# A chain of FNet and GeGLU layers on one core: two entries of the scheduler's machine picture are set in the source

## Chip, cores, metric

The kernel runs on one core of a Trainium2 chip. The metric is the device time of one execution, in microseconds; lower is better. Every program here is run several times, and the median counts.

The core's engines are TensorE (PE: matmuls; PEld: its weight loads), VectorE (DVE), ScalarE (ACT), GpSimd (POOL) and SyncE (SP, which issues transfers). Each works through its own queue in order and waits on semaphores for the others. Matmul results land in PSUM, of which this kernel uses 8 banks of 128 x 512; everything else on the core lies in SBUF.

## What is computed

An activation x of 2048 x 512 goes through four layers: FNet mixing, GeGLU, FNet mixing, GeGLU. All is float32.

```python
def _A_ref(x, dft_seq_re, dft_seq_im, dft_hid_re, dft_hid_im):
    a = jnp.einsum("bsd,ed->bse", x, dft_hid_re)
    b = jnp.einsum("bsd,ed->bse", x, dft_hid_im)
    return jnp.einsum("ts,bse->bte", dft_seq_re, a) - jnp.einsum("ts,bse->bte", dft_seq_im, b)

def _B_ref(x, w_gate, w_up, w_down):
    return (_gelu(x @ w_gate) * (x @ w_up)) @ w_down

x = x + _A_ref(_layernorm(x, axis=-1), A_dft_seq_re, A_dft_seq_im, A_dft_hid_re, A_dft_hid_im)
x = x + _B_ref(_layernorm(x, axis=-1), B_w_gate, B_w_up, B_w_down)
x = x + _A_ref(_layernorm(x, axis=-1), A_dft_seq_re, A_dft_seq_im, A_dft_hid_re, A_dft_hid_im)
x = x + _B_ref(_layernorm(x, axis=-1), B_w_gate, B_w_up, B_w_down)
```

The sequence matrices are 2048 x 2048, the hidden ones 512 x 512, and the feed-forward width is 1792.

## The kernel before

**Matmuls.** A float32 product is made of three reduced-precision ones. `split` (L137 to L139) cuts an operand into a high part, a copy on ACT (L138), and a low part, a subtraction on DVE (L139); `mm3` (L171 to L174) then adds high x high, high x low and low x high into one PSUM bank. So each 128 x 512 operand costs one ACT and one DVE instruction before its matmuls can run, the second matmul of three (or the third) needs the low part, and the first only the high part.

**Seven products for eight.** The big products are done on 2 x 2 blocks with seven block products (named A11, A12, S1 to S4 and A22 on one side, B.. and T1 to T4 on the other). This adds sums and differences on DVE (`plus` L163, `minus` L160), which work on loaded tiles before they are split and on PSUM banks when they are emptied. A bank is emptied by DVE (L163, adding to a tile) or by ACT (`copied`, L167); until then no later product may start in it.

**Tiles and loads.** 94 slots of 128 x 512 in SBUF hold everything in flight, with two wide tiles (`wide`, `xwide`) that are lent out as slots. SP issues nearly all loads in the order of its queue: the streamed matrices (L270, `ws` the sequence matrices, `wh` the hidden ones, `wc`, `wd`, `wdn` down weights), gate and up weights (`wgu` L845 to L847, their split copies `wb` L891), rows of x (L200, L209) and turned blocks `t` (L610). POOL issues the stores (L216, L227, L254, L863). A load into a slot waits until the last reader of the slot is done.

**Row statistics.** From the second layer on a row's mean and variance come from ACT (`norm_terms`: L492 sums a row, L493 the mean, L494 the squares), POOL (L495, L496) and ACT again (L497, and L514, which applies them). They share ACT's queue with the splits and the bank evacuations.

**What sets the order.** The source says what is done and in which program order, and which tile uses which slot. In what order each engine gets its instructions is decided by the tile framework's scheduler, which is called with `schedule_with_timeline_sim=True`: it plays the program through on a picture of the machine (a table of durations, the specification of the chip), and gives an engine that is free the first instruction in program order that is ready by that picture. The result is a fixed order for each queue, PE, ACT, DVE, POOL and SP alike. On the chip nothing of it is decided again: an instruction at the head of a queue that isn't ready holds up all behind it. Two entries of the picture matter here: `PE_FULL_CLOCK_PASS_GAP_NS`, the time between one pass over the array and the next beyond its columns, and `DGE_DMA_DELAY`, the time from the issue of a transfer to its start, with a value for each engine that issues.

Of the kernel before, what the change touches and what calls it, by code (L numbers as in the profile page):

```python
# [2 lines left out]

# [34 lines left out]
MADE = 5  # L38
LEAD = 3
NK = NS // 2  # L40


@with_exitstack
def fnet_geglu(ctx: ExitStack, tc: tile.TileContext, x_in, ws, wh, wgu, wdn, wdc, out):
# [153 lines left out]
    def x_load(layer, i, engine=nc.sync):  # L198
        t = sb.get()
        engine.dma_start(t, rows(layer, i))  # L200
        return t
# [116 lines left out]
    def make_a11(k):  # L318

        def run(v):  # L320
            held[k] = v
            return split_slot(v)
        return run
# [42 lines left out]
    def skewed(n):  # L366

        skew = SKEW[n - 2]
        return [(i, k - i * skew) for k in range(NK + (n - 1) * skew) for i in range(n) if 0 <= k - i * skew < NK]

# [14 lines left out]
    def bare(layer, b, what):  # L385

        return layer == 0 and b == 0 and what == "A11"
# [18 lines left out]
    def mix_items(layer):  # L406
        def raw(make, *tiles):
            items.append((F32, tiles, make, None))

        for b, what in plan(layer):  # L410
            tiles = [[ws[(b * 2 + m) * NS + k] for k in range(NS)] for m in range(2)]
            (a11, a12), (a21, a22) = ((r[:NK], r[NK:]) for r in tiles)
            hold = b >= FORE[layer]
            if what == "A11":
                for k in range(NK):
                    raw(as_is if bare(layer, b, what) else make_a11(k) if hold else plain, a11[k])
            elif what == "A12":
                for k in range(NK):
                    raw(plain, a12[k])
# [90 lines left out]
    def normed(layer, i, mixed=False):  # L510
        x = row_of(layer, i, mixed)
        z = sb.get()
        rstd, shift = known.pop((layer, i), None) or norm_terms(layer, i, x, z)
        nc.scalar.activation(z, x, AF.Identity, bias=shift, scale=rstd)  # L514
        sb.put(x)
        return z
# [11 lines left out]
    def first_rows(layer, k):  # L528
        for i in range(k if k == 0 else k + 2, min(k + 3, NK)):
            fresh[i] = x_load(layer, i)  # L530
        first_norm(layer, k)
        first_parts(k)

    def second_norm(layer, k):
        zb[k] = normed(layer, NK + k)

# [789 lines left out]
                geglu(w, layer)  # L1326


# [41 lines left out]
```

## Time and profile before

| | |
|---|---|
| runs shown | 1657.16, 1660.72, 1663.95 us (median 1660.72) |
| span of the profiled execution, first to last instruction | 1657.3 us |
| granted TensorE clock, mean | 0.994 |
| PE, PEld, DVE, ACT, POOL busy | 98%, 80%, 71%, 50%, 14% |
| matmuls of 128 x 512 in three parts | 2334 for each of the three lines of `mm3` |
| HBM read, written | 336.86 MB, 85.72 MB |

The profile is of one execution, and the time of that execution is its span and what lies around it, which the profile does not show; its span is as long as the shortest of the runs. Rows of the timeline give the start in microseconds, the duration, engine, line, operation, out<-in, and in brackets the idle time of the engine before it with what ended it. Names of tiles stand without their numbers: `p` is a PSUM bank, `s` a slot. "L163" is a line of the kernel, and often that of a helper, so many different sums share it. Records of matmuls overlap, so a matmul's duration in the profile is longer than the distance from its start to the next one's. A number in brackets behind a matmul is idle time only; time lost to a lower granted clock is read from tables of stretches.

### The profile page before, as it was taken

Reading aid. Unit: us, or ns where it says so; the run is one execution under the profiler, and the core shown is the slowest. Engines: PE = TensorE matmul, PEld = TensorE weight load, DVE = VectorE, ACT = ScalarE, POOL = GpSimd, SP = SyncE. Lnnn points to the kernel's source line nnn. Section 1 sums busy time; section 2 is a strip of 40 time slices with the busy share of each in tenths; the row PEclk is TensorE's granted clock in tenths of the full one; section 3 lists DMA queues with packets and bytes.
Section 4 is the critical chain, followed back from the end, with each engine's and each line's share of the span. In section 5 each row is a group of like instructions: output and inputs, shape, how many; then the busy total and the mean of one; then the engine's idle time right before and its main releaser. Section 6 shows DMA issues by size and latency. Waiting matters only on the chain.

```text
span 1657.3 us, 22815 instructions
## 1 busy us (share of the span) xinstructions
PE 1623.1 (98%) x7066; PEld 1329.5 (80%) x7066; DVE 1169.0 (71%) x2009; ACT 825.4 (50%) x1605; POOL 233.0 (14%) x421
## 2 busy tenths in 40 slices
PE   9999999989999999999999999999999999999998
PEld 6877888868788788888877888877778888788887
DVE  8998878769675674667877977787764556845573
ACT  7754454535675544555686433445345545523360
POOL 3111010202444113210030000101001000010002
PEclk9999999999999999999999999999999999999999
DMA  9768787789877799987867767777889775896455
GB/s 359 245 226 274 241 268 232 259 270 341 318 268 257 216 328 373 346 276 231 276 198 257 251 216 231 227 275 237 275 286 300 233 216 175 271 301 206 141 184 152
DMA packets 252106, 424.15 MB, mean 256 GB/s; under 512 B 28816, under 2 KB 91024, under 8 KB 250960
## 3 DMA queue, kind: packets, MB, share of 16 engines
q1 hardware_dynamic: 227232, 336.95, 63.9%
q0 software_dynamic: 24752, 85.74, 14.1%
q8 instruction: 56, 0.92, 0.2%
q14 instruction: 66, 0.54, 0.1%
HBM read 336.86 MB, written 85.72 MB: 255 GB/s over the span
## 4 chain that ended last, share of the span: by engine, by line
PE 76%; DMA 8%; DVE 7%; ACT 4%; issue 2%; SPq 1%; POOL 1%; DVEq 0%; ACTq 0%; POOLq 0%
PE p L172 25%; PE p L173 25%; PE p L174 25%; DVE s L139 3%; DMA s<-ws 3%; ACT s L138 2%; DVE s L160 2%; DMA s<-wgu 1%; DVE s L163 1%; DMA s<-x 1%; DMA s<-wdn 1%; DMA s<-t 1%; DMA t<-wide 0%; DMA begun<-wide 0%; ACT s L514 0%
## 5 line engine op out<-in xcount | busy, mean ns | idle before, releaser
L172 PE MATMUL p<-s,s 128*128 128x512 f32 x2334 | 891.6, 392 | 22.6 <-ACT s L138 8.4
L173 PE MATMUL p<-s,s 128*128 128x512 f32 x2334 | 911.3, 391 | 1.3 <-DVE s L139 1.3
L174 PE MATMUL p<-s,s 128*128 128x512 f32 x2334 | 901.0, 391 | 2.6 <-DVE s L139 2.5
L138 ACT ACTIVATE s<-s 128x512 fp32r<-128x512 f32 (+1 forms) x762 | 435.0, 606 | 452.6 <-DVE s L160 151.9
L139 DVE TENSOR_TENSOR s<-s,s 128x512 fp32r<-128x512 f32 (+1 forms) x762 | 483.2, 662 | 99.6 <-ACT s L138 77.7
L172 PEld LDWEIGHTS p<-s,s 128*128 128x128 f32 x2334 | 439.5, 188 | 122.6 <-ACT s L138 13.0
L174 PEld LDWEIGHTS p<-s,s 128*128 128x128 f32 x2334 | 440.2, 189 | 96.5 <-DVE s L139 3.8
L173 PEld LDWEIGHTS p<-s,s 128*128 128x128 f32 x2334 | 440.4, 189 | 94.5 <-DVE s L139 2.2
L163 DVE TENSOR_TENSOR s<-s,p 128x512 f32<-128x512 f32 x287 | 192.3, 682 | 169.9 <-PE p L174 74.1
L160 DVE TENSOR_TENSOR s<-s,s 128x512 f32<-128x512 f32 (+1 forms) x310 | 188.1, 620 | 47.3 <-DMA s<-ws 37.5
L167 ACT ACTIVATE s<-p 128x512 f32<-128x512 f32 x214 | 125.5, 592 | 113.5 <-PE p L174 105.9
L901 ACT ACTIVATE s<-s 128x512 f32<-128x512 f32 x103 | 64.6, 629 | 80.3 <-DVE s L163 79.4
L138 ACT ACTIVATE s<-xwide 128x512 fp32r<-128x512 f32 (+1 forms) x96 | 58.4, 615 | 46.9 <-DVE xwide L160 8.8
L163 DVE TENSOR_TENSOR s<-s,s 128x512 f32<-128x512 f32 (+1 forms) x70 | 43.0, 615 | 49.0 <-DMA s<-wgu 24.6
L495 POOL TENSOR_SCALAR rstd<-rstd 128x1 f32<-128x1 f32 x48 | 18.1, 378 | 406.7 <-ACT s L494 330.5
L139 DVE TENSOR_TENSOR s<-xwide,s 128x512 fp32r<-128x512 f32 (+1 forms) x96 | 64.5, 676 | 14.9 <-ACT s L138 12.7
L254 POOL DMA_DIRECT2D wb<-s x84 | 45.6, 545 | 56.4 <-ACT s L138 33.1
L915 DVE TENSOR_TENSOR s<-s,s 128x512 f32<-128x512 f32 x75 | 51.8, 690 | 1.9
L492 ACT ACTIVATE s<-s 128x512 f32<-128x512 f32 x39 | 24.4, 625 | 50.7 <-DMA s<-x 32.7
L514 ACT ACTIVATE s<-s,shift,rstd 128x512 f32<-128x512 f32 x55 | 43.9, 809 | 7.2 <-DVE shift L487 5.6
L216 POOL DMA_DIRECT2D x<-s x39 | 21.3, 546 | 171.8 <-DVE s L163 170.2
L596 DVE STREAM_TRANSPOSE wide<-s 128x512 f32<-128x512 f32 x30 | 21.1, 705 | 24.9 <-ACT s L514 19.3
(98 smaller groups left out, 530.7 us busy)
## 6 DMA issues: line engine op xcount, KB each, us to landing
s<-ws SPq DMA_DIRECT2D x379, 256.0 KB, 4.3
s<-wb SPq DMA_DIRECT2D x294, 256.0 KB, 4.8
s<-wc SPq DMA_DIRECT2D x119, 256.0 KB, 4.2
s<-wh SPq DMA_DIRECT2D x116, 256.0 KB, 4.3
wb<-s POOLq DMA_DIRECT2D x98, 256.0 KB, 4.5
s<-x SPq DMA_DIRECT2D x63, 256.0 KB, 5.0
xwide<-ws SPq DMA_DIRECT2D x58, 256.0 KB, 4.0
wc<-s POOLq DMA_DIRECT2D x49, 256.0 KB, 6.2
```

The source lines that it names most:

```text
L138: nc.scalar.activation(hi, src, AF.Copy)
L139: nc.vector.tensor_tensor(lo, src, f32(hi), op=ALU.subtract)
L160: nc.vector.tensor_tensor(out, a, b, op=ALU.subtract)
L163: nc.vector.tensor_tensor(out, a, b, op=ALU.add)
L167: nc.scalar.activation(v, src, AF.Copy)
L172: nc.tensor.matmul(ps, ah, bh, start=start, stop=False, skip_group_check=True)
L173: nc.tensor.matmul(ps, ah, bl, start=False, stop=False, skip_group_check=True)
L174: nc.tensor.matmul(ps, al, bh, start=False, stop=stop, skip_group_check=True)
L254: nc.gpsimd.dma_start(a, f32(t))
L514: nc.scalar.activation(z, x, AF.Identity, bias=shift, scale=rstd)
L901: nc.scalar.activation(t, g, AF.Gelu_apprx_tanh)
L915: nc.vector.tensor_tensor(t, t, v, op=ALU.mult)
```

## The change

While the scheduler orders the program, two entries of its picture are replaced, and put back afterwards: the gap between two passes of TensorE at full clock goes from 2.5 ns to 13.34 ns, and the delay of transfers issued by SP from 650 ns to 1900 ns (the other engines' stay as they are).

```diff
+PASS_GAP_NS = 13.34
+SP_DELAY_NS = 1900
...
+@contextmanager
+def machine_as_traced():
+
+    from concourse import hw_specs
+
+    spec = hw_specs.TRN2Spec
+    kept = {name: getattr(spec, name) for name in ("PE_FULL_CLOCK_PASS_GAP_NS", "DGE_DMA_DELAY")}
+    spec.PE_FULL_CLOCK_PASS_GAP_NS = PASS_GAP_NS
+    spec.DGE_DMA_DELAY = {**spec.DGE_DMA_DELAY, mybir.EngineType.SP: SP_DELAY_NS}
+    try:
+        yield
+    finally:
+        for name, value in kept.items():
+            setattr(spec, name, value)
...
-    with tile.TileContext(nc, schedule_with_timeline_sim=True) as tc:
+    with machine_as_traced(), tile.TileContext(nc, schedule_with_timeline_sim=True) as tc:
         fnet_geglu(tc, *ins, out)
```

The program has the same instructions on the same tiles and slots as before: 7,034 matmuls, 1,508 ACT, 2,009 DVE, 1,498 SP and 415 POOL instructions. Only their places in the queues differ. The lines of the kernel behind the two new constants are two further down than before, those from `kernel` on eighteen.

More of the change, by code (lines that the diff above doesn't have):

```diff
@@ L1 @@
 import math
-from contextlib import ExitStack
+from contextlib import ExitStack, contextmanager
 import concourse.bass as bass
```

## Prediction

> **What bounds the kernel now.** I read the page first: its span, the engines' busy shares, the chain that ended last, and the matmul groups.
>
> ```profile
> span 1657.3 us, 22815 instructions
> PE 1623.1 (98%) x7066; PEld 1329.5 (80%) x7066; DVE 1169.0 (71%) x2009; ACT 825.4 (50%) x1605; POOL 233.0 (14%) x421
> PE 76%; DMA 8%; DVE 7%; ACT 4%; issue 2%; SPq 1%; POOL 1%; DVEq 0%; ACTq 0%; POOLq 0%
> L172 PE MATMUL p<-s,s 128*128 128x512 f32 x2334 | 891.6, 392 | 22.6 <-ACT s L138 8.4
> L173 PE MATMUL p<-s,s 128*128 128x512 f32 x2334 | 911.3, 391 | 1.3 <-DVE s L139 1.3
> L174 PE MATMUL p<-s,s 128*128 128x512 f32 x2334 | 901.0, 391 | 2.6 <-DVE s L139 2.5
> ```
>
> TensorE is the bound. It makes 3 x 2,334 = 7,002 big matmuls and is idle for only 22.6 + 1.3 + 2.6 = 26.5 us in front of them. The mean of 391 ns is no pace, since records overlap; the pace is read from stretches. The next view is a table of stretches: its columns are PE, PEld, DVE, ACT and POOL busy with their instructions, then granted clock, DMA share and GB/s. The first row is undisturbed; the others begin where a stall had just ended.
>
> ```profile
> 200.00:250.00 50.00, 50.00 (x222) 41.41 (x221) 37.15 (x61) 24.66 (x55) 4.30 (x9) 1.00 0.80 270
> 349.00:353.00 4.00, 4.00 (x12) 3.14 (x11) 3.94 (x8) 1.71 (x4) 0.00 (x0) 0.57 0.56 163
> 372.80:376.20 3.40, 3.38 (x9) 2.64 (x10) 3.40 (x6) 1.42 (x3) 0.00 (x0) 0.55 1.00 329
> 430.20:434.60 4.40, 4.40 (x13) 3.46 (x14) 1.95 (x3) 1.26 (x3) 0.47 (x1) 0.61 0.68 238
> 542.30:547.20 4.90, 4.90 (x15) 3.86 (x16) 4.87 (x10) 3.34 (x7) 3.57 (x7) 0.65 1.00 270
> 870.90:878.00 7.10, 5.68 (x14) 4.16 (x15) 7.10 (x14) 7.10 (x15) 0.61 (x1) 0.54 0.48 153
> 1203.50:1207.00 3.50, 3.26 (x13) 2.39 (x14) 3.49 (x6) 0.63 (x1) 0.00 (x0) 1.00 0.88 309
> ```
>
> 50 us hold 222 matmuls, 225 ns each, so 7,002 of them need 1,577 us whatever their order. Behind five of the six long stalls the granted clock is 0.54 to 0.65 for some 4 us; one such drop costs (1 - 0.57) x 4.0 = 1.7 us. I use 1.7 us, and a chance of 5 in 6 that a stall of 1.9 us or more brings it. Five drops cost (1-0.57) x 4.0 + (1-0.55) x 3.4 + (1-0.61) x 4.4 + (1-0.65) x 4.9 + (1-0.54) x 7.1 = 10 us. A new order therefore has 26.5 + 10 = 36 us to win at most, 2.2% of the span, and no such limit on what it can lose.
>
> **The change part by part.** No instruction is added or removed. Comparing the two built programs instruction by instruction, 1,695 of 7,034 matmuls, 616 of 1,508 ACT, 910 of 2,009 DVE, 564 of 1,498 SP and 104 of 415 POOL instructions stand in another place of their engine's sequence, by 0.5 to 1.5 places in the mean. Queues run in order, so a moved instruction costs something only where its engine or its reader waits. I went through the stalls of TensorE one by one and took each engine's k-th place to be at the time of its k-th place before.
>
> Stalls that get shorter, in order of time:
>
> ```profile
> 95.28 0.50 PE L173 MATMUL p<-s,s 128*128 128x512 f32 x1 [1.03 <-DVE s L139]
> 483.54 0.73 PE L174 MATMUL p<-s,s 128*128 128x512 f32 x2 [0.99 <-DVE s L139]
> 542.25 0.50 PE L172 MATMUL p<-s,s 128*128 128x512 f32 x1 [2.66 <-DVE s L163]
> 870.88 0.75 PE L172 MATMUL p<-s,s 128*128 128x512 f32 x2 [3.46 <-ACT s L138]
> 873.05 1.22 PE L172 MATMUL p<-s,s 128*128 128x512 f32 x2 [1.42 <-ACT s L138]
> 1095.76 0.50 PE L172 MATMUL p<-s,s 128*128 128x512 f32 x1 [0.77 <-DVE s L163]
> 1415.22 0.50 PE L172 MATMUL p<-s,s 128*128 128x512 f32 x1 [0.56 <-ACT s L138]
> ```
>
> - 95.28: the low half waited for comes six places earlier on DVE, and the matmuls behind it go later: the whole 1.0 us.
> - 483.54: the two waiting matmuls move behind some fourteen that are ready: the whole 1.0 us.
> - 542.25: the evacuation waited for stands one place earlier, with one half-width subtraction less before it (two in 0.88 us, below): 0.4 us.
> - 870.88 and 873.05: the split waited for moves two places earlier on ACT, its low half one on DVE, and two matmuls of the second wait move back. Bounds 0 and 1.7 us (870.88 is 1.0 us earlier, and the next ready work 1.7); I take 0.7, because the second wait then begins sooner.
> - 1095.76: the evacuation (L163) moves one place forward, 0.6 us (five in 3.09 us at 1199.09, below).
> - 1415.22: two ready matmuls fill the gap: 0.5 us, and 0.3 us of a similar stall 6 us later.
>
> ```profile
> 540.72 0.88 DVE L160 TENSOR_TENSOR s<-s,s 128x256 f32<-128x256 f32 x2
> 541.52 0.68 DVE L163 TENSOR_TENSOR s<-s,p 128x512 f32<-128x512 f32 x1
> ```
>
> Together 1.0 + 1.0 + 0.4 + 0.7 + 0.6 + 0.5 + 0.3 = 4.5 us.
>
> Stalls that get longer. The first is at 137.40, where p waits for a PSUM bank that DVE empties with L163:
>
> ```profile
> 134.85 0.69 DVE L160 TENSOR_TENSOR s<-s,s 128x512 f32<-128x512 f32 x1 [1.00 <-DMA s<-ws]
> 136.66 0.68 DVE L163 TENSOR_TENSOR xwide<-s,p 128x512 f32<-128x512 f32 x1
> 137.40 0.50 PE L172 MATMUL p<-s,s 128*128 128x512 f32 x1 [1.31 <-DVE xwide L163]
> ```
>
> L163 moves three places back, behind three splits of other loads, at 0.60 us a place: 1.8 us. The bounds are 0.8 us (the 1.00 us that DVE idled at 134.85 is filled in the new order) and 1.8. I take 1.8, since two of those splits wait for loads of their own. The stall grows from 1.3 to 3.1 us, so a drop may follow: 5/6 x 1.7 = 1.4 us.
>
> The second is at 430.10. ACT empties two banks (L167) around a row statistic (L492) that waits for a load:
>
> ```profile
> 425.44 0.58 ACT L167 ACTIVATE s<-p 128x512 f32<-128x512 f32 x1
> 428.84 0.63 ACT L492 ACTIVATE s<-s 128x512 f32<-128x512 f32 x1 [2.19 <-DMA s<-x]
> 429.47 0.58 ACT L167 ACTIVATE s<-p 128x512 f32<-128x512 f32 x1
> 430.10 0.50 PE L172 MATMUL p<-s,s 128*128 128x512 f32 x1 [1.90 <-ACT s L167]
> ```
>
> In the new order the first L167 stands behind L492 as well, so it ends at 429.47 + 0.58 = 430.05, and the second goes behind the squares too. TensorE has six matmuls left from 424.6 on where it had thirteen: seven more are still to do at 430.1, 7 x 0.225 = 1.6 us. Late next are the six matmuls of that bank, which cover the second L167. The bounds are 0 (were the load early) and 2.6 (seven at the dropped clock, 3.40 / 9 = 0.38 us each in the stretch from 372.80). The drop itself is there already.
>
> The third is at 1203.43:
>
> ```profile
> 1198.48 0.69 DVE L160 TENSOR_TENSOR s<-s,xwide 128x512 f32<-128x512 f32 x1
> 1199.09 3.09 DVE L139 TENSOR_TENSOR s<-s,s 128x512 fp32r<-128x512 f32 x5
> 1202.70 0.68 DVE L163 TENSOR_TENSOR s<-s,p 128x512 f32<-128x512 f32 x1
> 1203.43 0.50 PE L172 MATMUL p<-s,s 128*128 128x512 f32 x1 [2.56 <-DVE s L163]
> 1192.74 0.33 SPq L270 DMA_DIRECT2D s<-ws  x1
> 1193.16 5.47 SPq L610 DMA_DIRECT2D s<-t  x8
> s<-ws SPq DMA_DIRECT2D x379, 256.0 KB, 4.3
> ```
>
> The load of 1192.74 moves behind the eight loads of t, to 1198.3. Its subtraction L160 moves three places back, to 1200.3, and would wait until 1198.3 + 4.3 = 1202.6; L163 comes five places behind it and also loses a place. So L163 is late by 0.6 us (if the load is back by 1200.3) to 0.6 + 2.3 = 2.9. I take 1.8, the middle: DMA is not crowded there. The stall becomes 4.4 us, and a drop that was spared before gets likely: another 1.4 us.
>
> Two more orders change with little at stake:
>
> ```profile
> 348.56 1.64 PE L172 MATMUL p<-s,s 128*128 128x512 f32 x4 [2.50 <-ACT s L138]
> 372.82 0.57 PE L172 MATMUL p<-s,s 128*128 128x512 f32 x1 [3.01 <-DVE xwide L163]
> ```
>
> At 348.56 two groups of six change places, one ready early and one late: between -1 and +1 us, I take 0. At 372.82 one matmul that ran ahead of the stall now comes behind it: 0.2 us.
>
> The other moves lie where a result is mostly ready two microseconds or more ahead of its matmul; the cover is the work queued on TensorE. Where it is thinner than the move, one more 0.6 us place is paid; I put 0 for it in the sum and let the range carry it.
>
> Losses: 1.8 + 1.4 + 1.6 + 1.8 + 1.4 + 0.2 = 8.2 us. Sum: 8.2 - 4.5 = +3.7 us on 1,657.3, which is 1,661.0. The three runs shown are 1,657.2, 1,660.7 and 1,664.0; the profiled span lies at their lower end, 3.4 below the median. On the median the sum gives 1,660.7 + 3.7 = 1,664.4 us, 0.2% more.
>
> Two rules of the Trainium skill speak to this. TensorE: Matmul & The Clock Gate, section "Wait — 56ns, not 53.3ns?", gives 215.7 ns from one warm 512-column matmul to the next. By it the old entry (2.5 ns of gap) would be right and the new one would make the picture of TensorE 7,002 x 10.8 ns = 76 us too long, which would raise the slower cases; the 222 matmuls of the first stretch, 225 ns each, speak for the new entry. The same page, in "Why this matters for your kernels", has the clock fall only behind gaps over about 3 us. By that estimate the first stall here (3.1) would be at the edge and 1.4 us might be saved; but this trace shows 0.61 behind 1.90 us, so the measurement decides and I keep 5 in 6.
>
> **The rivals.**
> - *Slower by more than 0.5%:* row statistics hold bank evacuations on ACT in more places. The loads of x are issued later in several places of the two feed-forward layers, and each L492 that waits holds the L167 behind it.
>
> ```profile
> ACT s L492 <- DMA s<-x: 32.7, 8, 12.1
> ```
>
>   Eight such waits, 4.1 us each; one of them is the stall at 430.10. It decides from the point where the wait outlasts the matmuls left over, about nine (2 us). Each further one costs 1.9 + 1.7 = 3.6 us; three more give 1,664.4 + 10.8 = 1,675. For it: the reordering is densest between 400 and 700. Against it: ACT is busy 50%, and in the places that I followed it came to the next L167 with time to spare.
> - *Faster by more than 0.5%:* the gains hold, the three longer stalls are absorbed because the loads come back in time, and three of the five drops are spared: -4.5 - 3 x 1.7 = -9.6, 1,651. For it: the picture's pace is now that of the trace. Against it: the evacuation order at 430.10 is plainly worse, whatever the loads do.
> - *Nothing happens* because the entries aren't read: excluded by the changed orders. That all effects cancel lies inside the forecast.
>
> **How the numbers follow.** About 0.5%, 8.3 us, is what a measurement of this kernel can tell from no change. The forecast (no change by that bound, 1,652.4 to 1,669.0) gets 0.5; the slower case, with its mechanism or with both new drops and thin covers elsewhere, 0.33; the faster 0.17. My sum's own bounds: losses all at their low end and no drop, 0.8 + 0 + 0.6 + 0.2 less gains of 5.5 and the 1 at 348.56, -4.9; all at their high end, 1.8 + 1.7 + 2.6 + 2.9 + 1.7 + 0.2 + 1 less gains of 3.8, +8.1. So 1,655.8 to 1,668.8 alone, and 3.4 more on each side for the spread of runs. Reaching out to both rivals: 1,651 to 1,676.
>
> **What would show it.** The new trace should have a stall of 3 us at about 137, one of 4 us before 430 with six matmuls of p behind it, one of over 4 us at about 1,205, and no stall at 95, 483 or 1,415. Wrong would be: no clock drop behind the first and third; evacuation waits on ACT between 440 and 700; or stalls at places where none was, since I priced those at nothing.

## The result and the profile after

The changed kernel took 1644.49 us in the median of four runs (1642.04 to 1646.90), the kernel before 1658.94 in the median of four (1655.79 to 1663.95). The ratio is 0.991, with a 95% interval of 0.9888 to 0.9932: 0.9% faster, where the forecast was no change by more than 0.5%, and 1,651 us was the low end of the range with both rivals.

The first lines are from the page of the kernel after: span, engines, the chain that ended last, and the matmul groups. In rows of this kernel `mm3` is L174 to L176, the split L140 and L141, differences L162, sums and DVE's bank evacuations L165, ACT's bank evacuations L169.

```profile
span 1642.2 us, 22851 instructions
PE 1618.0 (99%) x7066; PEld 1329.3 (81%) x7066; DVE 1169.2 (71%) x2009; ACT 827.5 (50%) x1605; POOL 229.2 (14%) x421
PE 79%; DVE 7%; DMA 6%; issue 2%; POOL 1%; ACT 1%; SPq 0%; DVEq 0%; POOLq 0%; ACTq 0%
L175 PE MATMUL p<-s,s 128*128 128x512 f32 x2334 | 909.8, 391 | 1.4 <-DVE s L141 1.4
L174 PE MATMUL p<-s,s 128*128 128x512 f32 x2334 | 893.6, 391 | 15.2 <-DVE s L165 7.9
L176 PE MATMUL p<-s,s 128*128 128x512 f32 x2334 | 900.4, 390 | 0.0
```

The busy times of DVE, ACT and POOL stand where they were. TensorE's idle time in front of the big matmuls fell from 26.5 to 15.2 + 1.4 = 16.6 us, and the share of the chain that runs through transfers from 8% to 6%. The span fell by 15.1, so about a third of it is not idle time. There are three stretches of lowered clock where there were five (columns as in the prediction):

```profile
363.14:369.97 6.83, 6.00 (x14) 4.68 (x15) 6.83 (x13) 4.83 (x9) 0.00 (x0) 0.50 0.85 274
854.65:861.48 6.83, 4.25 (x9) 2.95 (x10) 6.83 (x15) 6.83 (x16) 0.61 (x1) 0.50 0.40 137
1185.75:1192.58 6.83, 5.03 (x12) 3.96 (x13) 6.50 (x11) 2.14 (x4) 0.00 (x0) 0.50 0.82 254
```

They are longer than most of the old ones, though: 20.5 us together, as before (four of 3.41 us and one of 6.83). TensorE was busy in 15.3 us of them, before in 19.1, and at half clock that difference is worth only 1.9 us. Most of the rest goes with the number of stalls. Where a stall vanished whole, TensorE won some 0.3 us more than its idle time (1.33 us for the 1.03 at 95, 1.28 for the 0.99 at 483), and stalls over 0.2 us fell from 21 to 10, which is about 3 us by this estimate.

To find the places I set the start of the k-th matmul of one trace against the k-th of the other; both kernels have 7,066. The steps of that difference, by the time in the trace before:

| before, us | step, us | the prediction's term |
|---|---|---|
| start to 53 | -0.9 | 0 |
| 95 | -1.3 | -1.0 |
| 103 | -0.6 | 0 |
| 137 | -1.5 | +3.2 (1.8 and a drop) |
| 349 | -4.2 | 0 |
| 373 | +1.0 | +0.2 |
| 430 | -2.9 | +1.6 |
| 483 | -1.3 | -1.0 |
| 542 | -3.4 | -0.4 |
| 871 | -0.8 | -0.7 |
| 1076, 1096 | -1.1, -1.3 | 0, -0.6 |
| 1154 to 1173 | -1.4 | 0 |
| 1203 | +4.4 | +3.2 (1.8 and a drop) |
| 1415, 1422 | -1.0 | -0.8 |

With +0.2 elsewhere they add up, before rounding, to -16.0 at the last matmul; the end of the program behind it is 0.9 longer. The stalls at 95 and 483 are gone, as forecast; of those at 1415 and 1421 0.36 and 0.51 us are left (0.56 and 0.65 before). The one at 1203 grew, though by another route than forecast (below). What is wrong is four places, 137, 349, 430 and 542: forecast +4.4 together, measured -12.0. That is 16.4 us, and the whole miss in the span's change is -15.1 - 3.7 = -18.8.

At all four the chain of waits behind TensorE's stall ends in a load. Here are the rows of the kernel before that tell it: matmul and load at 137, then two rows at 349 (three loads of `ws` issued, and DVE's wait for one), then the four loads of x whose last one held the row statistic at 430, and DVE's wait for a load of `wgu` just ahead of the evacuation at 542.

```profile
131.62 0.39 PE L174 MATMUL p<-s,s 128*128 128x512 f32 x1
132.04 1.56 SPq L270 DMA_DIRECT2D s<-ws  x3
...
332.14 4.44 SPq L270 DMA_DIRECT2D s<-ws  x3
345.22 0.69 DVE L163 TENSOR_TENSOR s<-xwide,s 128x512 f32<-128x512 f32 x1 [7.37 <-DMA s<-ws]
...
418.75 5.26 SPq L209 DMA_DIRECT2D s<-x  x4
...
539.99 0.43 DVE L163 TENSOR_TENSOR s<-s,s 128x256 f32<-128x256 f32 x1 [6.25 <-DMA s<-wgu]
```

And the same instructions of the kernel after, with what hung on them:

```profile
122.03 0.39 PE L176 MATMUL p<-s,s 128*128 128x512 f32 x1
122.98 1.71 SPq L272 DMA_DIRECT2D s<-ws  x3
127.27 0.68 DVE L162 TENSOR_TENSOR s<-s,s 128x512 f32<-128x512 f32 x1
132.69 1.27 DVE L165 TENSOR_TENSOR xwide<-s,p 128x512 f32<-128x512 f32 x2
133.42 0.50 PE L174 MATMUL p<-s,s 128*128 128x512 f32 x1
...
325.39 2.83 SPq L272 DMA_DIRECT2D s<-ws  x2
336.83 0.69 DVE L165 TENSOR_TENSOR s<-xwide,s 128x512 f32<-128x512 f32 x1 [4.00 <-DMA s<-ws]
...
408.57 4.55 SPq L211 DMA_DIRECT2D s<-x  x4
418.57 0.61 ACT L494 ACTIVATE s<-s 128x512 f32<-128x512 f32 x1
419.81 0.50 PE L174 MATMUL p<-s,s 128*128 128x512 f32 x1 [0.82 <-ACT s L169]
...
526.78 0.42 DVE L165 TENSOR_TENSOR s<-s,s 128x256 f32<-128x256 f32 x1 [5.88 <-DMA s<-wgu]
```

At 137 the slot that the load of `ws` wants is last read by a matmul which the new order puts thirty places earlier on TensorE (place 505 to 475). It ran at 122.03 for 131.62, so the load started at 122.98 for 132.04, 9.1 us earlier. The difference L162 found it there and didn't wait, and the evacuation L165, though three places further back on DVE, began at 132.69 for 136.66. The stall of 1.31 us is gone.

At 349 and 430 the loads stand at the same places of SP's queue as before (the second of the three `ws` loads at place 319, those of x at 419 to 422), and still they start earlier: the second `ws` load, at 333.63 before, at 325.39, which is 8.2 us while TensorE was then only 4.2 ahead; those of x 10.2 us while TensorE was 7.4 ahead. The queue as a whole had moved forward: the slot of that `ws` load had been free since a matmul at 327.76, its last reader; what held the load until 333.63 were the loads ahead of it in SP's queue, which came 5 to 10 us earlier in the new order; one of them waits for a reader on DVE that ran at 321.58 for 329.49. DVE's wait for that load of `ws` fell from 7.37 to 4.00 us and the row statistic L494 at 418.57 no longer waited, so the two evacuations, which now both stand behind it and which I took to be held, came earlier too: TensorE's wait fell from 1.90 to 0.82 us. At 542 the load of `wgu` let DVE go on 13.2 us earlier (539.99 to 526.78) where TensorE was 11.8 ahead, and the stall fell from 2.66 to 0.76 us.

At 1203 the stall grew, but not by the forecast's mechanism. The load of `ws` does stand behind the eight loads of `t`, and the evacuation waits its turn on DVE:

```profile
1161.84 1.29 DVE L141 TENSOR_TENSOR s<-s,s 128x512 fp32r<-128x512 f32 x2 [3.08 <-DMA x<-s]
...
1174.77 0.69 DVE L162 TENSOR_TENSOR s<-s,s 128x512 f32<-128x512 f32 x1 [3.42 <-DMA s<-ws]
1174.80 6.15 SPq L612 DMA_DIRECT2D s<-t  x8
1181.06 0.38 SPq L272 DMA_DIRECT2D s<-ws  x1
1183.80 0.69 DVE L162 TENSOR_TENSOR s<-s,xwide 128x512 f32<-128x512 f32 x1
1186.82 1.27 DVE L165 TENSOR_TENSOR s<-s,p 128x512 f32<-128x512 f32 x2
1187.56 0.79 PE L174 MATMUL p<-s,s 128*128 128x512 f32 x1 [6.13 <-DVE s L165]
```

But the difference that reads this load, L162 at 1183.80, did not wait for it: DVE was busy without a break from 1180.66 to the evacuation. DVE had lost its lead before that. At 1157 it was 19.9 us ahead of its old times, about as far as TensorE (19.5). Up to 1174.77 it then waited 8.5 us for transfers (3.08 and 3.42 in the rows above, 0.84 and 1.17 between them), where the kernel before waited 4.3 in the same stretch. The evacuation came only 1202.70 - 1186.82 = 15.9 us earlier, and the stall grew by the difference, from 2.56 to 6.13 us. Of this the place that the evacuation lost on DVE is 0.6 us.

### The profile page after: what moved, and what is told of

It reads as the page before. It is cut to its first block, busy times and chain, and to the rows that moved or that the text cites. A ratio compares the mean times of both kernels' runs of the same rounds, so it can differ in the third digit from the quotient of the medians.

```text
span 1642.2 us, 22851 instructions
## 1 busy us (share of the span) xinstructions
PE 1618.0 (99%) x7066; PEld 1329.3 (81%) x7066; DVE 1169.2 (71%) x2009; ACT 827.5 (50%) x1605; POOL 229.2 (14%) x421
## 4 chain that ended last, share of the span: by engine, by line
PE 79%; DVE 7%; DMA 6%; issue 2%; POOL 1%; ACT 1%; SPq 0%; DVEq 0%; POOLq 0%; ACTq 0%
PE p L174 26%; PE p L175 26%; PE p L176 26%; DVE s L141 4%; DMA s<-ws 1%; DVE s L162 1%; DVE s L165 1%; DMA s<-t 1%; DMA s<-x 1%; DMA out<-s 1%; DMA xwide<-ws 1%; DMA s<-wgu 1%; DMA s<-begun 0%; DMA begun<-wide 0%; DMA begun<-xwide 0%
## 5 line engine op out<-in xcount | busy, mean ns | idle before, releaser
L174 PE MATMUL p<-s,s 128*128 128x512 f32 x2334 | 893.6, 391 | 15.2 <-DVE s L165 7.9
L176 PE MATMUL p<-s,s 128*128 128x512 f32 x2334 | 900.4, 390 | 0.0
L140 ACT ACTIVATE s<-s 128x512 fp32r<-128x512 f32 (+1 forms) x762 | 436.7, 607 | 459.0 <-DVE s L162 143.9
L141 DVE TENSOR_TENSOR s<-s,s 128x512 fp32r<-128x512 f32 (+1 forms) x762 | 482.6, 661 | 103.8 <-ACT s L140 70.3
L174 PEld LDWEIGHTS p<-s,s 128*128 128x128 f32 x2334 | 439.8, 188 | 113.0 <-DVE s L165 10.1
L176 PEld LDWEIGHTS p<-s,s 128*128 128x128 f32 x2334 | 439.9, 188 | 91.9 <-issue 0.2
L165 DVE TENSOR_TENSOR s<-s,p 128x512 f32<-128x512 f32 x287 | 192.4, 681 | 174.8 <-PE p L176 79.4
L162 DVE TENSOR_TENSOR s<-s,s 128x512 f32<-128x512 f32 (+1 forms) x310 | 187.2, 618 | 39.7 <-DMA s<-ws 29.9
L169 ACT ACTIVATE s<-p 128x512 f32<-128x512 f32 x214 | 124.8, 590 | 105.6 <-PE p L176 102.7
L140 ACT ACTIVATE s<-xwide 128x512 fp32r<-128x512 f32 (+1 forms) x96 | 58.6, 617 | 46.8 <-PE p L175 15.6
L141 DVE TENSOR_TENSOR s<-xwide,s 128x512 fp32r<-128x512 f32 (+1 forms) x96 | 64.4, 676 | 14.4 <-ACT s L140 12.2
L165 DVE TENSOR_TENSOR s<-s,s 128x512 f32<-128x512 f32 (+1 forms) x70 | 42.9, 614 | 36.3 <-DMA s<-wgu 19.9
L494 ACT ACTIVATE s<-s 128x512 f32<-128x512 f32 x39 | 24.4, 626 | 36.5 <-DMA s<-x 23.4
```

The lines of the kernel that those rows point to most:

```text
L140: nc.scalar.activation(hi, src, AF.Copy)
L141: nc.vector.tensor_tensor(lo, src, f32(hi), op=ALU.subtract)
L162: nc.vector.tensor_tensor(out, a, b, op=ALU.subtract)
L165: nc.vector.tensor_tensor(out, a, b, op=ALU.add)
L169: nc.scalar.activation(v, src, AF.Copy)
L174: nc.tensor.matmul(ps, ah, bh, start=start, stop=False, skip_group_check=True)
```

## The experiments

Two things had to be told apart: which of the two entries does it, and whether a truer picture makes a better order or any new order is a throw of dice. Each kernel is the changed one with other values of its two constants. They were run in four groups, each on one chip beside the kernel before, whose medians there were 1661.1, 1659.3, 1656.9 and 1660.8 us; ratios are to the kernel before of the same group.

**The two entries alone, a neighbour, and an overstated gap.**

```diff
# gap_only
-SP_DELAY_NS = 1900
+SP_DELAY_NS = 650
# delay_only
-PASS_GAP_NS = 13.34
+PASS_GAP_NS = 2.5
# both_2000
-SP_DELAY_NS = 1900
+SP_DELAY_NS = 2000
# gap25_1900
-PASS_GAP_NS = 13.34
+PASS_GAP_NS = 25
```

> Only the matmul gap is set (13.34 ns); the delay of SyncE's transfers stays at 650 ns. Theory A (the truer pace of TensorE makes the order: in the picture it no longer runs 5% ahead of its feeders, so the last readers of slots keep their places and loads start earlier): most of the gain is here, 1,645 to 1,650 us, and the stalls near 95, 137, 348 and 483 are gone. Theory B (the later landing of loads makes it): little gain, 1,655 to 1,661, and the stalls near 348 and 430, which end in late loads, remain. Theory C (any other order throws the dice again): anything from 1,640 to 1,670, with stalls at places where neither kernel has them.

> Only the delay of SyncE's transfers is set (1900 ns); the matmul gap stays at 2.5 ns. Theory A: little gain, 1,653 to 1,661 us. Theory B: most of the gain, 1,645 to 1,650, with the stalls near 348, 430 and 542 gone, which waited for loads of ws, x and wgu. Theory C: anything from 1,640 to 1,670, and the gains of the two single entries do not add up to the 14.5 us of both.

> Both entries, the delay of SyncE's transfers 100 ns longer (2000 ns). As a picture of the machine it is as true as the changed kernel's to within 100 ns; some 870 matmuls stand elsewhere. Theories A and B (a truer picture gives a better order): within 4 us of the changed kernel, 1,641 to 1,649 us. Theory C (dice): a difference from the changed kernel of the size of its gain is as likely as not, 1,635 to 1,665, and its largest stalls lie elsewhere.

> The matmul gap is overstated (25 ns, a pace of 237 to 239 ns in the picture where the trace has 225 to 227), the delay of SyncE's transfers stays at 1900 ns. Theory A (truth of the pace counts): as wrong as before's entry but on the other side, so the gain is lost again, 1,655 to 1,665 us. Rival D (a slower TensorE in the picture is better, true or not, because it brings loads and splits forward): still 1,640 to 1,650. Theory C: anything from 1,635 to 1,670.

Measured: the gap alone 1686.75 us (ratio 1.0159, 1.013 to 1.0188), the delay alone 1631.07 (0.9831, 0.9805 to 0.9857), both with 2000 ns 1639.75 (0.9875, 0.9846 to 0.9904), the gap of 25 ns 1669.54 (1.0057, 1.0033 to 1.0081). The two halves of the change pull against each other: the delay gains 30 us, the gap, alone, loses 26. Neither time lies in the range of any of the three theories. Theory A falls: the truer pace of TensorE is the half that loses. Theory B has the right half, though with more than twice the gain that it named, and it had no loss for the other. Its stalls go as it said: with the delay alone those near 348, 430 and 542 are gone, with the gap alone they remain, at 4.17, 3.43 and 4.59 us. The sum of the single effects, -4 us, is not the -14.5 of both. The neighbour with 2000 ns lies 4.7 us from the changed kernel, a little more than theories A and B allowed, but the intervals of the two overlap, so whether a throw of dice is in it isn't shown. The gap of 25 ns came out slower than any theory but the dice had it.

The waits of DVE for loads of `ws` and `wgu` in the kernel with the gap alone (columns: us in total, times, longest):

```profile
DVE s L162 <- DMA s<-ws: 41.5, 22, 7.0
DVE s L165 <- DMA s<-ws: 41.4, 18, 8.1
DVE s L165 <- DMA s<-wgu: 23.9, 9, 10.3
```

The same view of the kernel with the delay alone:

```profile
DVE s L162 <- DMA s<-ws: 28.5, 19, 6.1
DVE s L165 <- DMA s<-ws: 22.1, 13, 5.7
```

All rows of this view whose releaser is a transfer, added up, give DVE's idle time in front of loads: 153.0 us before, 137.8 after, 184.8 with the gap alone, 106.8 with the delay alone, 120.5 and 157.9 in the other two. That is the order of their times. What such a wait does to TensorE is seen in the timeline of DVE in the kernel with the gap alone:

```profile
255.51 1.42 DVE L162 TENSOR_TENSOR s<-s,s 128x512 f32<-128x512 f32 x2 [0.95 <-DMA s<-ws]
...
261.41 0.69 DVE L141 TENSOR_TENSOR s<-s,s 128x512 fp32r<-128x512 f32 x1
262.01 0.68 DVE L162 TENSOR_TENSOR s<-s,s 128x512 f32<-128x512 f32 x1
262.61 0.68 DVE L162 TENSOR_TENSOR xwide<-xwide,s 128x512 f32<-128x512 f32 x1
263.21 0.68 DVE L141 TENSOR_TENSOR s<-xwide,s 128x512 fp32r<-128x512 f32 x1
263.82 1.28 DVE L165 TENSOR_TENSOR s<-s,p 128x512 f32<-128x512 f32 x2
```

And of TensorE there:

```profile
252.61 0.39 PE L176 MATMUL p<-s,s 128*128 128x512 f32 x1
...
264.55 0.50 PE L174 MATMUL p<-s,s 128*128 128x512 f32 x1 [1.98 <-DVE s L165]
```

The matmul of 252.61 is the last of its bank. The evacuation that empties it, L165 at 263.82, comes eleven microseconds later, behind differences and splits of newly loaded tiles, one of which had waited for its load; the next product stands still for 1.98 us. In the kernel with the delay alone the same evacuation runs at 254.28 and its matmul at 260.85 without a wait. A bank is read by 568 instructions of the two evacuation helpers, and for 288 of them it is the last reading, behind which another product gets the bank. Those of the 288 that began more than 5 us behind the last matmul of their bank number 82 with the gap alone, 94 with the gap of 25 ns, 44 before, 31 after and 16 with the delay alone.

From this came theory E: in the picture of before loads land too early, so the scheduler puts instructions that need them at the heads of DVE's and ACT's queues, and on the chip they hold up evacuations that are ready.

**How the time goes with the delay.**

```diff
# delay_2000, delay_1275, delay_3200
-PASS_GAP_NS = 13.34
-SP_DELAY_NS = 1900
+PASS_GAP_NS = 2.5
+SP_DELAY_NS = 2000
# gap0_1900
-PASS_GAP_NS = 13.34
+PASS_GAP_NS = 0.0
```

(1275 and 3200 for 2000 in the second and the third.)

> The matmul gap as before (2.5 ns), the delay of SyncE's transfers 2000 ns, 100 more than in the run with the delay alone (1,631 us). Theory E (a later landing in the picture keeps instructions that would wait for loads off the heads of DVE's and ACT's queues; over the six kernels so far DVE's idle time in front of loads went 107, 121, 138, 153, 158, 185 us in the order of their times): 1,627 to 1,637 us, DVE idle for loads 100 to 118 us. Theory C (dice): 1,631 was a lucky order; this one lies at 1,640 to 1,660.

> The matmul gap as before (2.5 ns), the delay half-way between 650 and 1900 ns. Theory E: the effect grows with the delay, so between the two ends, 1,640 to 1,652 us, DVE idle for loads 115 to 145 us. Theory C: no order with the delay; outside 1,636 to 1,656 is as likely as inside.

> The matmul gap as before (2.5 ns), the delay 3200 ns, 1300 more than with the delay alone. Theory E, as long as the picture's loads still land earlier than the chip's (256 KB land 4.3 to 4.8 us behind their issue): the effect goes on but has less left to win (9.5 us of TensorE idle at 1,631), 1,620 to 1,632 us, DVE idle for loads under 107 us. Rival F (1900 ns was true and anything beyond it is as wrong as 650): 1,640 to 1,660. Theory C: anything from 1,625 to 1,665.

> The matmul gap 0 ns, further from the trace's pace than before's 2.5, the delay 1900 ns. Theory D' (a TensorE that is too fast in the picture orders better, since it is the bound on the chip and its feeders are then placed as early as they can be; at 1900 ns the times were 1,631 at 2.5 ns, 1,644 at 13.34, 1,670 at 25, 1.0 to 2.1 us for each ns): 1,627 to 1,633 us. Theory A (the truth of the pace counts): no better than 1,631, rather 1,633 to 1,640. Theory C: 1,625 to 1,655.

Measured: 1631.75 us (0.9836, 0.9819 to 0.9853), 1639.88 (0.9886, 0.9867 to 0.9905), 1630.40 (0.9826, 0.9809 to 0.9844) and 1631.78 (0.9835, 0.9818 to 0.9853), with DVE idle in front of loads for 109.9, 130.7, 77.5 and 93.6 us. The first three lie where theory E has them (1275 ns 0.1 us below its range). The dice (C) don't fit for this gap: four orders (1275, 1900, 2000 and 3200 ns) that each differ from before's in over a thousand matmuls follow the delay smoothly. For the gap of 0, 1631.78 lies in the range of theory D', but is no better than 1631.07 with 2.5 ns, so the line that was drawn from 25 over 13.34 to 2.5 ns ends there.

**One balance, or a harmful pace.** Why does the truer pace lose? If it is harmful in itself, it should lose at every delay. If what counts is only when loads stand ready beside products, the old entries erred on both sides, loads too early and products too early as well, and one error covered part of the other.

```diff
# both_3200
-SP_DELAY_NS = 1900
+SP_DELAY_NS = 3200
# both_4300
-SP_DELAY_NS = 1900
+SP_DELAY_NS = 4300
# delay_4300 (delay_0 has 0 for 4300)
-PASS_GAP_NS = 13.34
-SP_DELAY_NS = 1900
+PASS_GAP_NS = 2.5
+SP_DELAY_NS = 4300
```

> The matmul gap at 13.34 ns, the delay of SyncE's transfers 3200 ns. Theory G (one balance: what decides an order is when loads stand ready in the picture beside products of TensorE; before, loads came too early and products too early too, so setting TensorE's pace alone left loads further ahead; the longer delay closes that gap): the 25.6 us that the gap cost at 650 ns and the 13.4 at 1900 ns shrink to 0 to 7 at 3200, 1,630 to 1,637 us, DVE idle for loads under 105 us. Rival H (a slower TensorE in the picture orders worse in itself): again 12 to 14 us over the 1,630 of this delay alone, 1,640 to 1,646.

> The matmul gap at 13.34 ns, the delay 4300 ns. Theory G: no more than 4 us over the same delay with the gap as before, 1,627 to 1,635 us. Rival H: 10 us or more over it, 1,638 to 1,646.

> The matmul gap as before (2.5 ns), the delay 4300 ns: in the picture a transfer only starts when on the chip it has mostly landed. Theory E (saturated from 1900 ns on: 1,631, 1,632, 1,630): 1,625 to 1,632 us with DVE idle for loads under 90 us. Rival F (beyond the truth the order gets worse, since loads that are there are not used): 1,635 to 1,650, with ACT and DVE idle behind each other and not behind loads.

> The matmul gap as before (2.5 ns), the delay 0 ns, further from the chip than before's 650. Theory E: the slope between 650 and 1275 (20 us for 625 ns) goes on, 1,670 to 1,690 us, with DVE idle for loads above 165 us. Theory C (dice): 1,640 to 1,670.

Measured: 1633.49 us (0.9854, 0.9836 to 0.9873), 1628.05 (0.9825, 0.9804 to 0.9847), 1636.35 (0.9874, 0.9853 to 0.9896) and 1678.35 (1.0127, 1.0103 to 1.0151). The gap of 13.34 ns costs 25.6 us at a delay of 650, 13.4 at 1900, 3.1 at 3200 (where the two intervals overlap), and gains 8.3 at 4300. So the pace is not harmful in itself (rival H falls), and theory G holds, with more than it promised at 4300. For the gap of 2.5 ns the delay of 4300 is past the best, as rival F had it and theory E did not: 1636.35 is worse than 1630.40 by more than the intervals, though DVE's idle time in front of loads fell further, to 66.8 us. Nearly all of the difference lies at one place, where TensorE waits for a split on ACT, which had been busy for nine microseconds with hardly a pause:

```profile
856.22 1.22 PE L174 MATMUL p<-s,s 128*128 128x512 f32 x2 [5.15 <-ACT s L140]
```

The page of the kernel with 13.34 and 4300 ns shows what an order with about half the load waits looks like: 5.9 us of TensorE idle in front of the big matmuls, and 2% of the chain in transfers for 8% before.

```profile
span 1625.0 us, 22834 instructions
PE 93%; DVE 3%; DMA 2%; ACT 1%; issue 1%; POOL 0%; SPq 0%; DVEq 0%; POOLq 0%; ACTq 0%
L175 PE MATMUL p<-s,s 128*128 128x512 f32 x2334 | 907.3, 390 | 1.8 <-DVE s L141 1.8
L176 PE MATMUL p<-s,s 128*128 128x512 f32 x2334 | 897.6, 389 | 0.0
L174 PE MATMUL p<-s,s 128*128 128x512 f32 x2334 | 887.1, 390 | 4.1 <-ACT s L140 2.1
```

**The ends, and later loads on the chip itself.**

```diff
# gap25_4300
-PASS_GAP_NS = 13.34
-SP_DELAY_NS = 1900
+PASS_GAP_NS = 25
+SP_DELAY_NS = 4300
# slots92
-NSLOT = 94
-PASS_GAP_NS = 13.34
-SP_DELAY_NS = 1900
+NSLOT = 92
+PASS_GAP_NS = 2.5
+SP_DELAY_NS = 650
# slots92_both4300
-NSLOT = 94
-SP_DELAY_NS = 1900
+NSLOT = 92
+SP_DELAY_NS = 4300
# both_5000
-SP_DELAY_NS = 1900
+SP_DELAY_NS = 5000
```

> The matmul gap overstated (25 ns) with the delay at 4300 ns; at 1900 ns this gap took 1,669.5 us, 38 more than a gap of 2.5. Theory G (one balance: the delay moves loads back against products, the gap moves products back against loads): the longer delay makes most of it good, 1,632 to 1,645 us, with DVE idle for loads 90 to 120 us. Rival H (a slow TensorE in the picture orders worse whatever the delay): above 1,655.

> Both entries as before (2.5 and 650 ns), 92 slots for 94: every load waits for a slot that comes free later, so loads really land later while the picture's error stays. Theory E (the time goes with how long DVE's and ACT's heads wait for loads): slower than before by 5 to 25 us, 1,662 to 1,685, DVE idle for loads above 160 us. Theory that slots are no limit: within 4 us of before.

> 92 slots for 94, with the entries at 13.34 and 4300 ns (1,628 us with 94). Theory E: an order made for late loads has room for it, so it loses less than half of what the kernel before loses by the two slots: 1,629 to 1,640 us. Rival (two slots cost both orders alike): as much as the kernel before loses.

> The matmul gap at 13.34 ns, the delay 5000 ns. Theory G: the best delay for this gap lies near 4300, as the best for 2.5 lies between 1900 and 3200; 1,625 to 1,636 us. If longer were always better: under 1,624.

Measured: 1635.10 us (0.9832, 0.9806 to 0.9858), 1671.28 (1.0052, 1.0032 to 1.0073), 1639.51 (0.9858, 0.9833 to 0.9884) and 1630.16 (0.9807, 0.9781 to 0.9832). The gap of 25 ns, which cost 38 us at 1900, is nearly harmless at 4300: theory G again. With two slots fewer the kernel before lost 10.5 us by the medians and the order for late loads 11.5, but the latter compares two groups; by the ratios they lost 0.5% and 0.3%. I had expected less than half as much, the rival the same, and the intervals leave both open. As a test of cause this pair failed, since DVE's idle time in front of loads hardly moved (153.0 to 160.6 us, and 80.0 to 65.2): fewer slots did not delay the loads in the way meant. That late loads cause the stalls rests on the chains at single places and on the order of the times, not on a run that delays loads alone. Nor does a run separate what the new order of SP's queue does from what the new orders of DVE's and ACT's do.

Medians in us, over the whole field, with DVE's idle time in front of loads in brackets (the groups' kernels before differ by up to 4 us, so differences of that size between groups say little):

| delay, ns | gap 0 | gap 2.5 | gap 13.34 | gap 25 |
|---|---|---|---|---|
| 0 | | 1678 (186) | | |
| 650 | | before: 1659 (153) | 1687 (185) | |
| 1275 | | 1640 (131) | | |
| 1900 | 1632 (94) | 1631 (107) | after: 1644 (138) | 1670 (158) |
| 2000 | | 1632 (110) | 1640 (121) | |
| 3200 | | 1630 (78) | 1633 (79) | |
| 4300 | | 1636 (67) | 1628 (80) | 1635 (103) |
| 5000 | | | 1630 (76) | |

Several beat both kernels: the longer delay with either gap reaches ratios of 0.981 to 0.984 where the change has 0.991, and their intervals overlap too much to name one as the best.

## Why the prediction was wrong

**The step that failed** is "took each engine's k-th place to be at the time of its k-th place before". It holds for a queue that is never late, and here it was used for DVE and ACT, whose places are set by loads, and for loads, whose starts are set by the readers that release their slots. At 137 I saw that L163 moves three places back and priced them at 0.60 us each; the load behind it came 9.1 us earlier, which no place on DVE shows. At 430 I took the load of x to be back no earlier than before, so that L492 would start at 428.84 again, since the load's place on SP was the same; it was back in time because the queue ran earlier. At 349 and 542 it is the same with smaller moves. I had read "DMA 8%" in the chain, and the trace had waits of DVE for loads of up to 7.37 us, but I went on from TensorE's 26.5 us of idle time and followed each stall one step upstream.

**The gains** held in kind: 95, 483 and 1096 came out within 0.3 to 0.7 us of their terms, and 1415 within 0.2, though its stalls only shrank. 871 came out within 0.1, but by luck: its two stalls only went from 3.46 + 1.42 to 3.23 + 1.44 us, and the rest of the 0.8 came from the clock, since TensorE was busy in less of the half-clock stretch there (4.25 us for 5.40). 542 was sized at the one half-width subtraction that moved (0.4) and brought 3.4, since the stall fell from 2.66 to 0.76 us and the clock drop behind it went.

**The losses:** 137 and 430 had the wrong sign. 1203 was near in size, +4.4 for +3.2, and right in that a drop came (half clock for 6.83 us, in 5.0 of which TensorE was busy: 2.5 us for 1.4), but the mechanism was another: the load that I saw move was back in time, and DVE's waits for transfers ahead of it, not this load, made the stall 6.1 us. That the size was near is luck. 373 was 1.0 for 0.2.

**Moves priced at nothing** were not nothing: -0.9 at the start, -0.6, -1.1 and -1.4 at 103, 1076 and 1154 to 1173, all gains; none was a new stall. Two readings were off without bearing on the sum: from start to start the matmuls are 226.7 ns apart, not 225, since the 222 of the stretch count one that only reaches into it; and the time of an execution is some 1.9 us more than its span (1644.12 for 1642.2), so the profiled one was not 3.4 us below the median but about 1.5.

**The rivals.** The slower one, row statistics that hold evacuations in more places, did not come; the loads of x, which I took to be issued later, were issued earlier in time. The faster one is what happened, and in part by its own account: two of the three longer stalls were absorbed since loads came back in time, and three of five drops went, though a new one came at 1203 and the one at 373 grew to twice its length. But the argument for it was wrong: "the picture's pace is now that of the trace" is the half that loses 26 us alone. My remark on the 215.7 ns of the Trainium skill (TensorE: Matmul & The Clock Gate, section "Wait — 56ns, not 53.3ns?"), that the trace speaks for the new entry, is true of the pace (226.7 ns) and was no argument for the time. By that rule the old entry was right and the new one would raise the slower cases, which is what the gap alone did; the pace is not why, since a gap of 25 ns, still further off, is harmless once the delay is long.

**Dice or not.** I had put most of the chance on an outcome in which many small effects cancel. With the gap at 2.5 ns, five values of the delay from 0 to 2000 ns fall on one smooth line from 1678 to 1632 us; the effect was systematic, and a view that adds up DVE's waits for transfers (153 us) would have pointed to it.

## What to carry to other kernels

When a change reorders queues, don't hold the places at their old times: follow a stall upstream until it ends in something that no queue decides, here a load and the reader that frees its slot, and ask where that stands now. If a scheduler plays the program on a picture of the machine, errors of its entries can cover each other, so an entry that is corrected alone can lose; try it alone, together, and beyond the true value. Idle time of DVE and ACT in front of transfers is a number to watch even where TensorE is 98% busy, because such a wait can stand in front of evacuations that are ready. It is no full measure: the kernel with 2.5 and 4300 ns had 66.8 us of it and was 6 us slower than the one with 3200 ns and 77.5.

## What the runs showed of the hardware

Whether the clock falls behind a stall is not told by the stall's length. Before, 1.90 us at 430.10 was followed by half clock; in the kernel with 2.5 and 1275 ns a longer stall, here in the timeline of TensorE, was followed by the full clock:

```profile
422.56 0.73 PE L174 MATMUL p<-s,s 128*128 128x512 f32 x2 [2.91 <-DVE s L165]
```

What tells is how the idle time falls into windows. In the traces of all 18 kernels, the start and the end left out, every stretch of lowered clock has 0.50 and lasts 3.41 us or two or three times that, and within a kernel all of them begin on one grid with steps of 3.413 us. Cut along this grid, the kernel before shows around 430 and 1203:

```profile
427.73:431.14 3.41, 1.51 (x8) 0.91 (x7) 1.03 (x2) 2.27 (x7) 0.44 (x2) 1.00 1.00 353
431.14:434.55 3.41, 3.41 (x10) 2.65 (x9) 1.04 (x2) 0.32 (x1) 0.40 (x1) 0.50 0.63 225
1199.14:1202.55 3.41, 1.74 (x8) 1.12 (x6) 3.41 (x7) 2.54 (x5) 0.00 (x0) 1.00 0.34 99
1202.55:1205.96 3.41, 2.29 (x9) 1.60 (x10) 3.41 (x7) 1.28 (x3) 0.00 (x0) 1.00 0.83 270
```

And the kernel with 2.5 and 1275 ns:

```profile
417.98:421.39 3.41, 1.67 (x8) 1.06 (x6) 1.33 (x4) 0.63 (x1) 0.00 (x0) 1.00 1.03 399
421.39:424.81 3.42, 2.25 (x10) 1.87 (x11) 3.25 (x8) 2.92 (x8) 2.15 (x4) 1.00 0.77 207
```

The 1.90 us at 430 lie whole in one window, TensorE is busy in 1.51 us of it, and the next window has half the clock. The 2.91 us of the other kernel are split over two windows, with 1.74 and 1.17 us of idle time, and so are the 2.56 at 1203 (1.67, and 1.12 with two short stalls behind): no drop. Over the 18 traces, all 51 full-clock windows with 1.8 us or more of idle time had half clock behind them, none of those with less than 1.68 had, and three of the five between. So here a drop came when about half a window was idle, and whether a stall of 1.9 us brought one depended on where it fell. The prediction's 5 in 6 stood for this.

The Trainium skill, TensorE: Matmul & The Clock Gate, section "What's actually happening", has the gate look at windows of about 3.4 us that run free of the program. The traces agree, with steps of 3.413 us.
